# Low parts of split weights and sums of pooled values move from GpSimd to VectorE

## The chip, the core and the metric

The kernel runs on one core of one Trainium2 chip. The metric is the device time of one execution in microseconds (us), the median of several runs. The profile's names are used for the engines: PE is TensorE, DVE is VectorE, ACT is ScalarE, POOL is GpSimd, SP is SyncE, which here issues all DMAs.

## The reference

Three stages follow one another: an attention with two branches over 4 x 8 heads of 576 tokens, and two feed-forward layers over the 2304 tokens of width 512.

```
q_d, k_d, v_d = means over each 4 tokens of q, k, v        # 144 pooled tokens
out_up    = repeat(softmax(q_d k_d^T / 8) v_d, 4)
out_local = softmax(q k^T / 8 where |i - j| < 4) v
x = (out_up + out_local) as [2304, 512]
...
h = x @ w_in                       # moe1, 512 -> 1024
solu = h * softmax(h)
ln = (solu - mean) / sqrt(var + 1e-6) * g_ln
x = ln @ w_out                     # 1024 -> 512
...
h = x @ w_in                       # moe2, 512 -> 2048
out = (h * cos(h)) @ w_out         # 2048 -> 512
```

The four weight matrices arrive as float64, everything else as float32.

## The kernel before

**Products.** The feed-forward products run with float32r operands. Each operand is kept as a high part (its rounded value) and a low part (what is left), and `mm3` makes three matmuls of each product: high by high, high by low, low by high. `split(hi, lo, src, eng)` makes both parts: ACT copies `src` into the high part (line 355), and one subtraction makes the low part (line 356). The subtraction is on DVE, except where `eng=nc.gpsimd` is given, which is so for all four weights.

**Weights on their way in.** `wload` takes a block of a weight by DMA as 64-bit words and makes float32 of it with three integer operations on DVE (lines 393, 395 and 397): the raw words lie in tile `X` (first two weights, blocks of 512 columns) or `wr` (last two weights, blocks of 256 columns), the float32 block in `wu`, a ring of two. Then `split` puts the parts into `R1` (named `R` in the profile: both weights of moe1, later the second weight of moe2) or into `w2i_h` and `w2i_l`. There are 16 blocks of moe1's weights (`w1i_step`, `w1o_step`) and 64 of moe2's (`w2i_step`, `w2o_step`). In `w1o_step` POOL multiplies the block by the layer norm's weight and by 32, the root of 1024 (line 417), before the split.

**Attention.** `Glob` is the pooled branch of a pair of heads, `Loc` the banded one of 192 tokens of a pair. `Glob.prep` sums q and k over four tokens on DVE (line 479) and v on POOL: three additions (line 482) of 72 x 256 elements into `gvs`, 16 times in all. Scores go to PSUM, `softmax` (lines 433 to 440) works on DVE and ACT, PE transposes, and PE multiplies with the values. `Loc.V` adds both branches into `X` on DVE (line 561).

**moe1 and moe2.** `h1_half` is moe1's first product with a maximum on DVE (line 589; two for each 128 tokens, 36 in all), `h1_ln` the softmax and layer norm (its power -1/2 runs on POOL, line 616), `ln_t` the transposes with a split on DVE, `x2` the second product. moe2 goes through 9 groups of 256 tokens and 16 blocks of 128 columns: `h2` (product, cosine in lines 792 to 799, split), and two blocks later `o2`, which adds to the output's banks.

**Order.** The code states what waits for what, and `arrange` then sets the order in which every engine runs its instructions: a list schedule over the whole program on built-in estimates of durations, tried over 14 rounds. Its estimates take each engine by itself. At run time each engine takes its instructions strictly in that order. SP issues DMAs in order as well, so a load that waits for its buffer holds those behind it. `WARM` = 70 matmuls that nobody reads fill gaps of PE at the beginning.

In time, the attention and moe1's weights share the beginning; moe1 and the rest of the attention follow; moe2's weights are brought in alongside the last third of moe1 and the first group of moe2; then moe2 runs alone.

Of the kernel before, what the change touches and what calls it, by code (L numbers as in the profile page):

```python
# [18 lines left out]
FAC = 4              # tokens of a pooled token  # L19
HALO = FAC - 1       # half width of the band  # L20
QB = 64              # queries of a block
WIN = QB + 2 * HALO  # keys of a local block
NB = 3               # blocks of an item
QT = NB * QB         # tokens of a local item
GT = 256             # tokens of a MoE group
W1C, W2C = 512, 256  # columns of the weights' blocks on their way in

# How far, in items, an attention item's steps lie apart: its loads before its scores (a local item's,
# a global one's q and k, its v), its transposes and its values after them.
LEAD, LEAD_QK, LEAD_V, LAG_T, LAG_V = 2, 2, 1, 1, 2  # L30
PACE = 1.1           # steps of moe1 for each attention item
SIDE = 0.55           # blocks of moe1's weights for each attention item
LAG, RING = 2, 4     # moe2: blocks from the first product to the second, places for what lies between
WARM = 70            # matmuls that may fill the tensor engine's first gaps
ROUNDS = 14
# PSUM banks by what they hold
# [5 lines left out]
# ------------------------------------------------------------------------ order of the instructions  # L42
# A list schedule on estimates of what the instructions take settles the order in which each engine runs them.

TO_PE, TO_POOL, TO_ANY = 210.0, 180.0, 135.0  # ns from an engine to another
WRITTEN = {"DVE": 127.0, "Activation": 143.0, "Pool": 127.0}  # from a write to its read by the same engine
DMA_ISSUE, DMA_START, DMA_END, DMA_RATE, DMA_FLIGHT = 475.0, 1100.0, 935.0, 360.0, 8
CLOCK_TICK, CLOCK_COLUMNS = 10240 / 3, 3060.0  # the tensor engine's clock doubles after a tick with so many columns
# [3 lines left out]
class Turns:  # L52
    """A tile pool that keeps account of the tiles that take turns in its slots."""
# [27 lines left out]
def region(o):  # L81
    """An operand's tile, partitions and bytes."""
# [11 lines left out]
class Step:  # L94
    """An instruction, and what it is estimated to take."""
# [205 lines left out]
def kernel(  # L301
# [218 lines left out]
    class Loc:  # L520
# [32 lines left out]
        def V(self):  # L553
            ps = bank("lv")[:, :QT]
            for a in range(NB):
# [10 lines left out]
                op=ALU.add,  # L566
            )

    # --------------------------------------------------------------------- MoE 1
    H = {}  # L570
    TB = 128 // QB  # blocks of 128 tokens

# [314 lines left out]
```

## Time and profile before

| | |
|---|---|
| median of 3 runs | 826.56 us |
| the runs | 819.25, 826.56, 827.91 us |
| span of the profiled execution | 816.9 us |
| time of the profiled execution | not listed; 819.25 us if it was the first run, which leaves 2.4 us outside the span |
| PE busy | 792.9 us, 97% |
| DVE busy | 528.0 us, 65% |
| ACT busy | 473.3 us, 58% |
| POOL busy | 130.6 us, 16% |

The busy shares are means over stages with different limits, so the stretches matter more than the whole. A busy time counts each moment once; the durations of single instructions can overlap a little, since the next one on an engine may begin before the last one's record ends. POOL's spans are rough.

### The profile page before, as it was taken

The numbers are of one execution on the slowest core, as the hardware profiler recorded it, in microseconds if no ns is written. First come the engines' busy times: TensorE is split into PE (matmuls) and PEld (weight loads), VectorE is DVE, ScalarE is ACT, GpSimd is POOL, SyncE is SP. The second block draws the span as 40 slices with busy tenths as digits, with TensorE's granted clock in tenths as the row PEclk, the third lists the DMA queues.
The fourth block names the chain that finished last, engine by engine and source line by source line (L and its number), as shares of the span: only waits on it lengthen the run. The fifth ranks groups of instructions, "written<-read, shape, count | busy, mean of one in ns | idle before, by whom it ended". The sixth has DMA issues, their size and how long they took to land.

```text
span 816.9 us, 15396 instructions
## 1 busy us (share of the span) xinstructions
PE 792.9 (97%) x5894; PEld 672.2 (82%) x5894; DVE 528.0 (65%) x1348; ACT 473.3 (58%) x1366; POOL 130.6 (16%) x172
## 2 busy tenths in 40 slices
PE   6898999999999999999999999999999999999998
PEld 3565768787787887998978999999999999999997
DVE  6987997775747478889999544444445445454443
ACT  3555566665637445455566656565656656565654
POOL 4473342220000013433333000000000000000000
PEclk9977999999999999999999999999999999999999
DMA  9964520401200023332432000000000000000000
GB/s 253 238 167 142 149 76 23 158 17 34 70 18 28 12 68 115 104 116 85 137 116 91 27 1 26 1 27 1 26 2 1 27 1 26 1 27 1 26 1 26
DMA packets 23481, 50.34 MB, mean 62 GB/s; under 512 B 3792, under 2 KB 7664, under 8 KB 23408
## 3 DMA queue, kind: packets, MB, share of 16 engines
q1 hardware_dynamic: 23408, 49.36, 19.6%
q8 instruction: 46, 0.75, 0.4%
q14 instruction: 27, 0.22, 0.1%
HBM read 44.63 MB, written 4.72 MB: 60 GB/s over the span
## 4 chain that ended last, share of the span: by engine, by line
PE 76%; DVE 16%; issue 3%; DMA 2%; ACT 1%; POOL 1%; SPq 0%; POOLq 0%; DVEq 0%; ACTq 0%
PE h2b L361 4%; PE h2b L360 4%; PE h2b L359 4%; PE h2a L360 4%; PE ob L361 4%; PE h2a L359 4%; PE oa L359 4%; PE ob L360 4%; PE oa L360 4%; PE h2a L361 4%; PE ob L359 4%; PE oa L361 4%; PE ls L541 3%; DVE wu L395 3%; PE h L359 3%
## 5 line engine op out<-in xcount | busy, mean ns | idle before, releaser
L356 DVE TENSOR_TENSOR Gl<-t,Gh 128x256 fp32r<-128x256 f32 x144 | 61.5, 427 | 55.8 <-ACT Gh L355 55.8
L355 ACT ACTIVATE Gh<-t 128x256 fp32r<-128x256 f32 x144 | 60.0, 417 | 58.5 <-DVE t L797 58.3
L795 ACT ACTIVATE t<-t 128x256 f32<-128x256 f32 x144 | 60.1, 418 | 55.8 <-DVE t L793 55.6
L359 PE MATMUL x<-Gh,R 128*128 128x256 f32 x288 | 81.8, 286 | 1.7 <-ACT Gh L355 1.5
L360 PE MATMUL x<-Gl,R 128*128 128x256 f32 x288 | 81.8, 285 | 0.7 <-DVE m L596 0.4
L361 PE MATMUL x<-Gh,R 128*128 128x256 f32 x288 | 81.9, 286 | 0.0
L797 DVE SCALAR_TENSOR_TENSOR t<-t,h2b 128x256 f32<-128x256 f32 x72 | 30.2, 420 | 58.2 <-ACT t L796 58.2
L797 DVE SCALAR_TENSOR_TENSOR t<-t,h2a 128x256 f32<-128x256 f32 x72 | 30.2, 420 | 54.2 <-ACT t L796 54.1
L796 ACT ACTIVATE t<-t 128x256 f32<-128x256 f32 x144 | 60.2, 418 | 4.2
L359 PE MATMUL h<-R,xh 128*128 128x512 f32 x144 | 62.3, 433 | 0.3 <-ACT xh L355 0.3
L361 PE MATMUL h<-R,xl 128*128 128x512 f32 x144 | 59.6, 415 | 0.0
L360 PE MATMUL h<-R,xh 128*128 128x512 f32 x144 | 59.0, 410 | 0.0
L359 PE MATMUL oa<-R,Gh 128*128 128x512 f32 x144 | 57.4, 399 | 1.6 <-ACT Gh L355 1.6
L361 PE MATMUL oa<-R,Gl 128*128 128x512 f32 x144 | 56.5, 392 | 1.7 <-DVE Gl L356 1.7
L359 PEld LDWEIGHTS x<-Gh,R 128*128 128x128 f32 x288 | 55.0, 191 | 3.2 <-ACT Gh L355 2.0
L361 PE MATMUL ob<-R,Gl 128*128 128x512 f32 x144 | 57.1, 397 | 0.0
L360 PE MATMUL oa<-R,Gh 128*128 128x512 f32 x144 | 56.9, 395 | 0.0
L360 PEld LDWEIGHTS x<-Gl,R 128*128 128x128 f32 x288 | 55.1, 191 | 2.1 <-DVE Gl L356 1.4
L360 PE MATMUL ob<-R,Gh 128*128 128x512 f32 x144 | 56.6, 393 | 0.0
L436 ACT ACTIVATE le<-ls,sm 128x70 f32<-128x70 f32 x144 | 44.2, 319 | 21.0 <-DVE sm L434 12.2
L359 PE MATMUL ob<-R,Gh 128*128 128x512 f32 x144 | 56.3, 391 | 0.0
L361 PEld LDWEIGHTS x<-Gh,R 128*128 128x128 f32 x288 | 55.0, 191 | 1.0 <-issue 0.6
(120 smaller groups left out, 2284.8 us busy)
## 6 DMA issues: line engine op xcount, KB each, us to landing
wr<-in_w2i_dram SPq DMA_DIRECT2D x32, 256.0 KB
wr<-in_w2o_dram SPq DMA_DIRECT2D x32, 256.0 KB
lv<-in_vl_dram SPq DMA_DIRECT2D x48, 105.0 KB
gv<-in_vg_dram SPq DMA_DIRECT2D x16, 288.0 KB
out_dram<-X SPq DMA_DIRECT2D x18, 256.0 KB
X<-in_w1i_dram SPq DMA_DIRECT2D x8, 512.0 KB
X<-in_w1o_dram SPq DMA_DIRECT2D x8, 512.0 KB
kt<-in_k_dram SPq DMA_DIRECT2D x6, 594.0 KB
```

Of the source, the lines that this page charges most:

```text
L355: nc.scalar.activation(out=hi, in_=src, func=AF.Copy)
L356: (eng or nc.vector).tensor_tensor(out=lo, in0=src, in1=hi.bitcast(F32), op=ALU.subtract)
L359: nc.tensor.matmul(ps, lh, rh, start=start, stop=False)
L360: nc.tensor.matmul(ps, lh, rl, start=False, stop=False)
L361: nc.tensor.matmul(ps, ll, rh, start=False, stop=stop)
L395: nc.vector.scalar_tensor_tensor(out=ui, in0=high, scalar=-0x40000000, in1=ui, op0=ALU.bitwise_and, op1=ALU.bitwise_or)
L436: nc.scalar.activation(out=e[:, j, :], in_=src[:, j, :], func=AF.Exp, bias=neg[:, j:j + 1], scale=scale, accum_out=ssum[:, j:j + 1])
L541: nc.tensor.matmul(o[64 * h:64 * h + 64, :], self.q[:, h, a * QB:(a + 1) * QB], self.k[:, h, a * QB:a * QB + WIN], start=False, stop=a == ...
L795: nc.scalar.activation(out=a, in_=c, func=AF.Sin, scale=0.5)
L796: nc.scalar.activation(out=c, in_=a, func=AF.Square, scale=2.0 ** 0.5)
L797: nc.vector.scalar_tensor_tensor(out=a, in0=c, scalar=1.0, in1=ps, op0=ALU.subtract, op1=ALU.mult, reverse0=True)
```

## The change

Everything that POOL did with two-input arithmetic on large tiles goes to DVE; of the arithmetic POOL keeps only the power of the layer norm.

- The low parts of all 80 weight blocks are made on DVE (`split` no longer has an `eng`).
- In `w1o_step` the multiplication of the block by the layer norm's weight (line 417) is dropped as an instruction. `split` takes the weight as `gain`: ACT copies with a scale per partition, and DVE makes the low part as (src x gain) - high in one instruction. The factor 32 is put into `g_sb` once, by one small DVE instruction.
- The sum over four v tokens becomes two additions on DVE: tokens 0, 1 plus tokens 2, 3 in place (72 x 512 elements), then the two halves (72 x 256).

The rest of the difference removes comments only. Line numbers after the change are four to six higher: 355 becomes 356 (or 359 with a gain), 356 becomes 357 (or 360), 393, 395, 397 become 398, 400, 402, and 482 becomes 485 and 487.

```diff
-    def split(hi, lo, src, eng=None):
-        nc.scalar.activation(out=hi, in_=src, func=AF.Copy)
-        (eng or nc.vector).tensor_tensor(out=lo, in0=src, in1=hi.bitcast(F32), op=ALU.subtract)
+    def split(hi, lo, src, gain=None):
+
+        if gain is None:
+            nc.scalar.activation(out=hi, in_=src, func=AF.Copy)
+            nc.vector.tensor_tensor(out=lo, in0=src, in1=hi.bitcast(F32), op=ALU.subtract)
+        else:
+            nc.scalar.activation(out=hi, in_=src, func=AF.Copy, scale=gain)
+            nc.vector.scalar_tensor_tensor(out=lo, in0=src, scalar=gain, in1=hi.bitcast(F32),
+                                           op0=ALU.mult, op1=ALU.subtract)
...
     def w1i_step(i):
-        split(w1i_h[:, k, f], w1i_l[:, k, f], wload(w1i[k * 128:(k + 1) * 128, f], stage), eng=nc.gpsimd)
+        split(w1i_h[:, k, f], w1i_l[:, k, f], wload(w1i[k * 128:(k + 1) * 128, f], stage))
...
         u = wload(w1o[k * 128:(k + 1) * 128, f], stage)
-        nc.gpsimd.tensor_scalar(out=u, in0=u, scalar1=g_sb[:, k:k + 1], scalar2=DFF ** 0.5, op0=ALU.mult, op1=ALU.mult)
-        split(w1o_h[:, k, f], w1o_l[:, k, f], u, eng=nc.gpsimd)
+        split(w1o_h[:, k, f], w1o_l[:, k, f], u, g_sb[:, k:k + 1])
...
-            for r in range(1, FAC):
-                nc.gpsimd.tensor_tensor(out=vs, in0=self.v[:, :, 0, :] if r == 1 else vs, in1=self.v[:, :, r, :],
-                                        op=ALU.add)
+            nc.vector.tensor_tensor(out=self.v[:, :, 0:2, :], in0=self.v[:, :, 0:2, :], in1=self.v[:, :, 2:4, :],
+                                    op=ALU.add)
+            nc.vector.tensor_tensor(out=vs, in0=self.v[:, :, 0, :], in1=self.v[:, :, 1, :], op=ALU.add)
...
     nc.sync.dma_start(out=g_sb, in_=gln.rearrange("(k p) -> p k", p=128))
+
+    nc.vector.tensor_scalar(out=g_sb, in0=g_sb, scalar1=DFF ** 0.5, scalar2=None, op0=ALU.mult)
...
-        split(w2i_h[:, kk, f], w2i_l[:, kk, f], wload(w2i[kk * 128:(kk + 1) * 128, f], raw2), eng=nc.gpsimd)
+        split(w2i_h[:, kk, f], w2i_l[:, kk, f], wload(w2i[kk * 128:(kk + 1) * 128, f], raw2))
...
-            split(w2o_s[:, j, 0, f], w2o_s[:, j, 1, f], wload(w2o[j * 128:(j + 1) * 128, f], raw2), eng=nc.gpsimd)
+            split(w2o_s[:, j, 0, f], w2o_s[:, j, 1, f], wload(w2o[j * 128:(j + 1) * 128, f], raw2))
```

Since `arrange` plans the whole program anew, the order moves on every engine. Two places matter here. At the beginning, while moe1's first weight comes in, this is POOL's order before (`gvs` and `gv` are the pooled values' sums and their raw tokens, `wu` a float32 block):

```order
L482 TENSOR_TENSOR gvs_298<-gv_271 72x256
L482 TENSOR_TENSOR gvs_298<-gvs_298,gv_271 72x256 x2
L356 TENSOR_TENSOR R1_70<-wu_213,R1_70 128x512
L356 TENSOR_TENSOR R1_70<-wu_258,R1_70 128x512
L482 TENSOR_TENSOR gvs_423<-gv_371 72x256
L482 TENSOR_TENSOR gvs_423<-gvs_423,gv_371 72x256 x2
L356 TENSOR_TENSOR R1_70<-wu_315,R1_70 128x512
```

After the change the same work stands in DVE's order, between the conversions of the next blocks (lines 398 to 402) and the softmax's small steps (`sm`):

```order
L400 SCALAR_TENSOR_TENSOR wu_259<-X_71,wu_259 128x512
L357 TENSOR_TENSOR R1_70<-wu_214,R1_70 128x512
L398 TENSOR_SCALAR wu_314<-X_71 128x512
L442 TENSOR_SCALAR sm_477<-sm_477 128x2
L402 SCALAR_TENSOR_TENSOR wu_259<-X_71,wu_259 128x512
L485 TENSOR_TENSOR gv_370<-gv_370 72x2x256
L485 TENSOR_TENSOR gv_418<-gv_418 72x2x256
L487 TENSOR_TENSOR gvs_422<-gv_370 72x256
L487 TENSOR_TENSOR gvs_442<-gv_418 72x256
L443 RECIPROCAL sm_477<-sm_477 128x2
```

Each low part stands several instructions behind the conversion of its own block, and the sums stand in pairs. The second place is the first group of moe2, while its second weight comes in. DVE's order before:

```order
L393 TENSOR_SCALAR wu_5592<-wr_5593 128x256
L797 SCALAR_TENSOR_TENSOR t_5414<-t_5414,h2b_5444 128x256
L395 SCALAR_TENSOR_TENSOR wu_5592<-wr_5593,wu_5592 128x256
L397 SCALAR_TENSOR_TENSOR wu_5592<-wr_5593,wu_5592 128x256
L356 TENSOR_TENSOR Gl_73<-t_5414,Gh_72 128x256
L793 SCALAR_TENSOR_TENSOR t_5499<-t_5499,h2a_5486 128x256
```

And the order of DVE in the same place after the change:

```order
L400 SCALAR_TENSOR_TENSOR wu_5314<-wr_5315,wu_5314 128x256
L398 TENSOR_SCALAR wu_5322<-wr_5323 128x256
L803 SCALAR_TENSOR_TENSOR t_5217<-t_5217,h2a_5204 128x256
L402 SCALAR_TENSOR_TENSOR wu_5314<-wr_5315,wu_5314 128x256
L799 SCALAR_TENSOR_TENSOR t_5217<-t_5217,h2b_5247 128x256
L357 TENSOR_TENSOR Gl_73<-t_5217,Gh_72 128x256
L400 SCALAR_TENSOR_TENSOR wu_5322<-wr_5323,wu_5322 128x256
L357 TENSOR_TENSOR R1_70<-wu_5314,R1_70 128x256
L402 SCALAR_TENSOR_TENSOR wu_5322<-wr_5323,wu_5322 128x256
```

Here the low part of a block (`R1_70<-wu_5314`) stands three instructions behind the last conversion of that block (line 402), and the next block's conversion has begun ahead of it.

## Rows read from the trace of the kernel before

**Rows 1.** The page: the span and the busy times.
```profile
span 816.9 us, 15396 instructions
...
PE 792.9 (97%) x5894; PEld 672.2 (82%) x5894; DVE 528.0 (65%) x1348; ACT 473.3 (58%) x1366; POOL 130.6 (16%) x172
```

**Rows 2.** Busy us (and instructions) in four stretches, then granted clock, DMA share, GB/s.
```profile
15.00:127.50 112.50, 104.17 (x927) 68.99 (x926) 102.84 (x261) 63.94 (x250) 52.61 (x58) 0.89 0.55 156
127.50:300.00 172.50, 172.50 (x1636) 138.55 (x1636) 109.73 (x341) 98.47 (x355) 16.25 (x24) 1.00 0.14 46
300.00:376.00 76.00, 74.16 (x489) 66.89 (x489) 67.58 (x170) 38.90 (x89) 28.51 (x36) 1.00 0.33 108
376.00:451.00 75.00, 71.17 (x490) 64.27 (x489) 71.80 (x171) 47.20 (x119) 26.63 (x35) 1.00 0.32 106
```

**Rows 3.** Groups on POOL: busy us, mean ns of one, idle before.
```profile
L356 POOL TENSOR_TENSOR w2i_l<-wu,w2i_h 128x256 fp32r<-128x256 f32 x32 | 26.1, 824 | 44.5 <-ACT w2i_h L355 44.4
L482 POOL TENSOR_TENSOR gvs<-gvs,gv 72x256 f32<-72x256 f32 x32 | 26.0, 813 | 1.9
...
L356 POOL TENSOR_TENSOR R<-wu,R 128x512 fp32r<-128x512 f32 x16 | 21.3, 1331 | 17.3 <-ACT R L355 17.3
```

**Rows 4.** Timeline about 397 us, all engines: start us, us, instruction.
```profile
396.37 0.28 DVE L393 TENSOR_SCALAR wu<-wr 128x256 int32<-128x256 int32 x1
...
396.69 0.42 DVE L395 SCALAR_TENSOR_TENSOR wu<-wr,wu 128x256 int32<-128x256 int32 x1
...
396.99 0.73 POOL L356 TENSOR_TENSOR R<-wu,R 128x256 fp32r<-128x256 f32 x1 [1.60 <-ACT R L355]
...
397.15 0.85 DVE L397 SCALAR_TENSOR_TENSOR wu<-wr,wu 128x256 int32<-128x256 int32 x1
...
397.93 0.28 DVE L393 TENSOR_SCALAR wu<-wr 128x256 int32<-128x256 int32 x1
```

**Rows 5.** Timeline about 48 us, in the attention.
```profile
47.83 1.27 POOL L356 TENSOR_TENSOR R<-wu,R 128x512 fp32r<-128x512 f32 x1
48.09 1.04 DVE L438 TENSOR_SCALAR sm<-sm 128x3 f32<-128x3 f32 x1
```

**Rows 6.** Timeline of DVE at the eighth maximum of moe1 (line 589).
```profile
126.85 0.68 DVE L589 TENSOR_REDUCE m<-h 128x1 f32<-128x512 f32 x1
```

**Rows 7.** Groups on DVE from 0 to 140 us.
```profile
L397 DVE SCALAR_TENSOR_TENSOR wu<-X,wu 128x512 int32<-128x512 int32 x16 | 14.6, 911 | 0.0
L395 DVE SCALAR_TENSOR_TENSOR wu<-X,wu 128x512 int32<-128x512 int32 x16 | 12.7, 794 | 0.0
L440 DVE TENSOR_TENSOR le<-le,sm 128x210 f32<-128x210 f32 x20 | 11.6, 578 | 0.1
L438 DVE TENSOR_SCALAR sm<-sm 128x3 f32<-128x3 f32 x26 | 11.4, 439 | 3.6 <-ACT le L436 3.4 <-ACT ge L436 0.2
...
L438 DVE TENSOR_SCALAR sm<-sm 128x2 f32<-128x2 f32 x4 | 3.2, 810 | 0.0
```

**Rows 8.** Groups on DVE from 180 to 298 us, where POOL has little to do.
```profile
L440 DVE TENSOR_TENSOR le<-le,sm 128x210 f32<-128x210 f32 x21 | 7.9, 376 | 0.6
...
L438 DVE TENSOR_SCALAR sm<-sm 128x3 f32<-128x3 f32 x25 | 4.1, 164 | 9.1 <-ACT le L436 7.8 <-ACT ge L436 1.3
...
L356 DVE TENSOR_TENSOR xl<-X,xh 128x512 fp32r<-128x512 f32 x5 | 3.4, 680 | 0.0
```

**Rows 9.** Groups on DVE from 300 to 450 us.
```profile
L397 DVE SCALAR_TENSOR_TENSOR wu<-wr,wu 128x256 int32<-128x256 int32 x64 | 34.6, 545 | 0.8
L395 DVE SCALAR_TENSOR_TENSOR wu<-wr,wu 128x256 int32<-128x256 int32 x63 | 29.4, 472 | 1.1
L393 DVE TENSOR_SCALAR wu<-wr 128x256 int32<-128x256 int32 x62 | 23.7, 386 | 6.4 <-POOL w2i_l L356 4.9 <-DMA wr<-in_w2i_dram 0.9 <-POOL R L356 0.6
```

**Rows 10.** Waits of the whole span: us in total, times, longest.
```profile
DVE Gl L356 <- ACT Gh L355: 58.1, 120, 0.7
...
SPq L469 <- POOL gvs L482: 17.1, 6, 6.4
```

## The prediction

> **What bounds the kernel now.** Start with the busy times: PE is busy for 792.9 of 816.9 us, DVE for 528.0, POOL for 130.6 [rows 1]. Read by itself this says that PE is the bound and that DVE has room. The table by stretch says otherwise [rows 2]. From 127.5 to 300 us PE is busy all 172.5 us and DVE only 109.7: there PE sets the pace. From 15 to 127.5 us DVE is busy 102.84 of 112.5 us, from 300 to 376 us 67.58 of 76, from 376 to 451 us 71.80 of 75. In the last two PE leaves 1.84 and 3.83 us unused, and in the first its granted clock is 0.89 on the mean, that is, it spent some time at the lower of its two levels (1.2 instead of 2.4 GHz). So DVE sets the pace in the beginning and nearly so while moe2's weights come in. Those two stretches are the places to which the change adds DVE work.
>
> The next view is the timeline, with DVE and POOL side by side. At 396.99 us a subtraction starts on POOL and takes 0.73 us, to 397.72. The conversion that starts on DVE at 397.15 takes 0.85 us; the one before it, with as many elements and also two tensor inputs, took 0.42 [rows 4]. At 47.83 us POOL starts one of 1.27 us, to 49.10; a DVE instruction on three columns starts at 48.09 and ends at 49.13, with POOL, after 1.04 us [rows 5]. So a DVE instruction that begins under a POOL instruction waits until POOL is through. What DVE loses in this way is counted as busy, which is why DVE looks full where POOL works.
>
> The Trainium skill, "SBUF — State Buffer", section "SBUF: two separate sides", says that DVE and GpSimd share a pair of SBUF ports as an exclusive lock: whoever starts first has it for its whole instruction, against DVE instructions in a two-port mode or with two SBUF inputs, and the other blocks. The two places above agree. By that rule alone the loss could be as large as POOL's 130.6 busy us; the sum below counts what the groups show, which is a third of it.
>
> **The change part by part.**
>
> *What DVE gets back at the beginning.* Compare DVE's groups up to 140 us [rows 7] with the same shapes where POOL is nearly idle [rows 8]: line 397, 16 x (911 - 680) = 3.7 us, with the 512 columns and two inputs of the `xl` row as the clean value; line 395, 16 x (794 - 680) = 1.8; line 440, 20 x (578 - 376) = 4.0; line 438, 26 x (439 - 164) = 7.2 and, on two columns, 4 x (810 - 164) = 2.6. These are 19.3 us. Other groups, line 393 among them, are stretched too and not counted; I take 22, with 19 and 25 as ends.
>
> *What DVE gets there.* The place that ends this stretch is the eighth maximum of moe1, at 126.85 + 0.68 = 127.5 us [rows 6]. In the new order all 16 low parts of moe1's weights and eight of the 16 pairs of value sums stand ahead of it on DVE. Low parts: 16 x 680 ns = 10.9 us [rows 8]. The multiplication by the gain is in the same pass, like the conversions of lines 395 and 397, so no more than that. Sums: 512 columns at 680 ns and 256 at 420 [rows 4, 8], 8 x 1.10 = 8.8 us. Together 19.7 us. A DVE instruction that waits for nothing starts about 0.07 us before the last one's record ends (397.15 + 0.85 against 397.93 [rows 4]), which is 2.2 us for 32 instructions. Net: 19.7 - 2.2 - 22 = **-4.5 us**, with ends of -7.5 and +0.7 (25 back and all of the overlap; 19 back and no overlap). The other eight pairs come where DVE is idle for 63 of 172.5 us [rows 2]: nothing, unless that room goes, when they cost 8.8 us.
>
> *The second weights.* Back, from 300 to 450 us: line 397, 64 x (545 - 420) = 8.0; line 395, 63 x (472 - 420) = 3.3; line 393, 62 x (386 - 280) = 6.6 [rows 9], with the clean values of the timeline [rows 4]: 17.9 us, and some more in shapes not shown. Added: 64 low parts x 420 ns, less 0.07 of overlap each, = 22.4 us. From 376 us on, a block takes 397.93 - 396.37 = 1.56 us on DVE, of which 0.43 is the block by POOL [rows 4]; afterwards it takes 1.56 - 0.43 + 0.35 = 1.48. For 32 blocks that is **-2.6 us**. From 300 to 376 us the other 32 add 11.2 us and get back what is left, 17.9 - 13.8 = 4.1 or somewhat more: 5 to 7 us more on DVE. That is covered by the 8.4 us in which DVE is idle there [rows 2]: 0, and up to +7 if the idle time lies in the wrong places. So the subtraction costs DVE hardly more by doing it than it cost DVE by waiting for POOL.
>
> *What else moves.* A subtraction or addition on POOL took 0.73 to 1.33 us [rows 3, 4], so whatever waits for a low part or a sum gets it earlier. The multiplication of line 417 goes from the path of a block of moe1's second weight; the scale on ACT's copy and the small instruction on `g_sb` I cost at nothing, covered by POOL's missing step; without that cover it is one short instruction on DVE. The pooled values' next load waits on SP for the sums (17.1 us in 6 waits [rows 10]), and behind it stand loads of local values and raw weights. It waits for DVE from now on; sums late in DVE's order would make those loads late. SP has such waits today without PE standing still from 127.5 us on, so 0, with up to +3 in the beginning.
>
> *The plan.* The order is planned on clean durations. Today DVE falls behind it by every blocked instruction, and engines in fixed order then wait for one another: DVE is idle for 9.7 us from 15 to 127.5 us, and PE for 5.7 us from 300 to 451 us [rows 2]. Afterwards the run should keep closer to its plan. How much of these 15.4 us returns no row tells; I take **-3**, with 0 and -15 as ends.
>
> The sum is -4.5 - 2.6 - 3 = -10.1 us. The page lists no time of its own for the profiled execution, only its span of 816.9 us; the lowest of the runs, 819.25, fits it best, and the median is 826.56. I put the change against the median: **816.5 us**. What lies outside the span I leave as it is.
>
> **The rivals.**
>
> *Faster still.* Most of the divergence from the plan goes: -4.5 - 2.6 - 15 = -22 us, 804.5 us. For it: the lower clock between 15 and 127.5 us belongs to the same stalls. Against: loads and scores have waits of their own there, which POOL has no part in.
>
> *No change.* What DVE gains at the beginning is taken by another limit: by PE, which was granted a mean clock of 0.89 there and whose work was merely shifted, or by loads. Only what PE has done when it becomes the bound at 127.5 us counts in the end. Then -0 to -3 us remain: 824 to 829 us.
>
> *Slower: DVE waits for ACT.* POOL could wait for ACT's copy of a block; DVE now stands in that place, and everything behind it on DVE waits too: softmax steps, `Gl`, the next conversions, and PE behind them. The comparable wait of today, DVE's `Gl` for ACT's `Gh`, takes 58.1 us in 120 times, 0.48 each [rows 10]. For 64 low parts this would be 31 us, less the 1.4 to 3.4 us of idle time that is left in the first of the two stretches; with the gain of 10 that gives about 845 us. It decides from some 0.2 us for each low part. Against it: in the new order at least two instructions stand between the last conversion of a block and its low part, in all but 2 of 64 cases.
>
> *Slower: DVE's work was worth sparing.* If the stretched records had another reason than POOL, nothing would come back: +17.5 us less 9.7 idle at the beginning, +22.4 less 8.4 and 3.2 later, +18.6 in all, 845 us. The ends that fall together with POOL's speak against it [rows 4, 5]. The Trainium skill, "Perfetto Trace Analysis", section "Optimizing Scalar/DVE Operations", advises to give work of a saturated DVE to ACT or even GpSimd, which speaks against this change, and adds that for GpSimd the shared read port may undo the gain. By its first half the time would be this rival's.
>
> **How the numbers follow.** The forecast, 811 to 822 us, gets 0.45; faster still 0.14; no change 0.26; DVE waiting for ACT 0.11; no blocking 0.04. About 1% (8.3 us) is what a measurement of this kernel can tell from no change, so faster means below 818.3 us: two thirds of the forecast's range, 0.29, and the second case, 0.43 in all. Slower means above 834.8: 0.15. The rest is 0.42. The range that leaves out both slower cases and the far tail of the fast one is 804 to 831 us.
>
> **What would show it.** In the new profile POOL's busy time falls to under 20 us, and DVE's stays within 15 us of 528: 10.9 + 16 x 1.10 + 64 x 0.42 = 55 us come on top, 8 of them in overlap, and 40 or more go. Lines 398, 400 and 402 have means near 280, 420 and 420 ns on 256 columns and 680 for the two on 512; line 442 has one near 164 ns from the start. The eighth maximum of moe1 (line 593 now) ends near 122 us, and PE is idle for less than 5.7 us while moe2's weights come in. If DVE waits for ACT's copies by more than some 0.2 us each, the third rival was right. If the eighth maximum comes earlier and the end does not, the second was. The largest unknown is the return of the plan: clock levels at the beginning can move it by several us either way.

## The result, and the profile after

The first comparison gave a median of 801.16 us after the change (four runs, 797.35 to 803.61) against 827.14 before (four runs, three of them from 826.56 to 827.91): a ratio of 0.9715, 95% interval 0.9652 to 0.9777. My range ended at 804.

Three more comparisons of the same two kernels came with the experiments, each on another chip: 0.9891 (0.984 to 0.9941), 0.9842 (0.9801 to 0.9884) and 0.9805 (0.9759 to 0.9852). In all, 22 runs after the change have a median of 803.9 us (797.26 to 813.64). 109 runs of the kernel before, beside the experiments, have one of 818.2 us (809.52 to 834.91), and only 6 of the 109 reach 826.5. Without the 12 of all these runs that lie over 1.5% above the fastest beside them, the medians are 803.9 and 817.9 us. So the change is worth about 14 us, and the first comparison showed the kernel before at its slow end.

The page after, as [rows 1]:

```profile
span 801.4 us, 15354 instructions
...
PE 783.0 (98%) x5894; PEld 669.9 (84%) x5894; DVE 523.4 (65%) x1461; ACT 473.0 (59%) x1366; POOL 18.2 (2%) x36
```

POOL lost 112 us of work. DVE took over 113 instructions more and is busy 4.6 us less. The same stretches as [rows 2] (busy us and instructions of PE, PEld, DVE, ACT and POOL; granted clock; DMA share; GB/s):

```profile
15.00:127.50 112.50, 105.24 (x982) 74.17 (x980) 96.87 (x288) 66.73 (x251) 1.48 (x2) 0.93 0.48 141
127.50:300.00 172.50, 172.50 (x1644) 137.97 (x1639) 119.45 (x377) 100.28 (x362) 6.70 (x9) 1.00 0.19 58
300.00:376.00 76.00, 76.00 (x515) 69.88 (x514) 71.17 (x205) 40.77 (x92) 5.56 (x7) 1.00 0.33 103
376.00:451.00 75.00, 75.00 (x517) 69.77 (x516) 66.67 (x197) 50.52 (x134) 0.00 (x0) 1.00 0.35 107
```

PE no longer stands still from 300 to 451 us, and it runs 1032 matmuls there where it ran 979. DVE's groups from 0 to 140 us (answering to [rows 7]) have the clean values now:

```profile
L402 DVE SCALAR_TENSOR_TENSOR wu<-X,wu 128x512 int32<-128x512 int32 x16 | 10.7, 682 | 0.0
L400 DVE SCALAR_TENSOR_TENSOR wu<-X,wu 128x512 int32<-128x512 int32 x16 | 10.7, 676 | 0.0
...
L444 DVE TENSOR_TENSOR le<-le,sm 128x210 f32<-128x210 f32 x20 | 7.4, 371 | 0.0
...
L485 DVE TENSOR_TENSOR gv<-gv 72x512 f32<-72x512 f32 x10 | 6.8, 679 | 3.0 <-DMA gv<-in_vg_dram 3.0
...
L360 DVE SCALAR_TENSOR_TENSOR R<-wu,g_sb,R 128x512 fp32r<-128x512 f32 x8 | 5.8, 744 | 0.0
L357 DVE TENSOR_TENSOR R<-wu,R 128x512 fp32r<-128x512 f32 x8 | 5.5, 682 | 1.0 <-ACT R L356 1.0
...
L442 DVE TENSOR_SCALAR sm<-sm 128x3 f32<-128x3 f32 x27 | 4.3, 161 | 3.7 <-ACT le L440 3.5 <-ACT ge L440 0.2
```

And from 300 to 450 us (answering to [rows 9]):

```profile
L402 DVE SCALAR_TENSOR_TENSOR wu<-wr,wu 128x256 int32<-128x256 int32 x60 | 25.0, 419 | 0.0
L400 DVE SCALAR_TENSOR_TENSOR wu<-wr,wu 128x256 int32<-128x256 int32 x60 | 24.9, 420 | 0.4
L398 DVE TENSOR_SCALAR wu<-wr 128x256 int32<-128x256 int32 x60 | 17.3, 289 | 2.0 <-DMA wr<-in_w2i_dram 1.3 <-DMA wr<-in_w2o_dram 0.3
L357 DVE TENSOR_TENSOR R<-wu,R 128x256 fp32r<-128x256 f32 x32 | 13.3, 419 | 0.1
L357 DVE TENSOR_TENSOR w2i_l<-wu,w2i_h 128x256 fp32r<-128x256 f32 x29 | 12.1, 418 | 0.4 <-ACT w2i_h L356 0.4
```

The last column settles a rival at once: in this stretch the low parts waited for ACT's copies for 0.1 + 0.4 us in all, not for 0.2 us each.

**Where the time went.** Two events divide the span: the 24th maximum of moe1 (lines 589 and 593) and the output copy that ends the second group of moe2 (lines 812 and 818). In between moe2's weights come in. The timelines give before:

```profile
297.99 0.69 DVE L589 TENSOR_REDUCE m<-h 128x1 f32<-128x512 f32 x1 [0.16 <-PE h L361]
...
499.37 0.58 ACT L812 COPY X<-ob 128x512 f32<-128x512 f32 x1
```

and after:

```profile
291.85 0.68 DVE L593 TENSOR_REDUCE m<-h 128x1 f32<-128x512 f32 x1
...
483.59 0.58 ACT L818 COPY X<-ob 128x512 f32<-128x512 f32 x1
```

The ends are 298.68 and 499.95 us before, 292.53 and 484.17 after. So the stretch between them fell from 201.3 to 191.6 us (**-9.6**), and the one ahead of it from 298.7 to 292.5 (**-6.2**). Behind it both kernels take the same time to 0.3 us. The stretch between the two events, before and then after (columns as in [rows 2]):

```profile
298.68:499.95 201.27, 195.60 (x1298) 176.84 (x1297) 163.98 (x398) 117.94 (x286) 55.14 (x71) 1.00 0.25 83
...
292.53:484.17 191.64, 191.64 (x1296) 176.90 (x1295) 161.08 (x461) 116.09 (x286) 5.56 (x7) 1.00 0.28 87
```

PE is busy in all of it after the change, at the full clock: there it is the bound. Before, it idles for 5.7 us and is busy 4.0 us longer with as many matmuls (a few records are missing). DVE runs 63 instructions more after the change and is busy 2.9 us less.

The first stretch differs from run to run, the second hardly: the three other profiled executions of the changed kernel have 191.4, 191.5 and 191.6 for the second, and 293.5, 297.7 and 286.8 for the first. Every experiment is read by these two. The ratios are those of the comparisons; a difference given with an experiment below is worked out from its ratio and 818.2 us. (For the first three parts the plain differences of medians, against 819.29 us beside them, are 1.6 to 2.4 us larger.)

| kernel | median us | ratio to before (95%) | to the 24th maximum | from there to the second output |
|---|---|---|---|---|
| before | 818.2 | | 298.7 | 201.3 |
| before again | 817.88 | 0.9997 (0.9964 to 1.003) | 313.3 | 201.3 |
| after | 803.9 | 0.9715, 0.9891, 0.9842, 0.9805 | 292.5 | 191.6 |
| before, moe2's low parts moved | 808.6 | 0.9896 (0.9845 to 0.9948) | 298.1 | 191.4 |
| before, moe1's low parts moved | 814.3 | 0.9968 (0.9938 to 0.9998) | 293.0 | 200.3 |
| before, sums moved | 808.8 | 0.9892 (0.9858 to 0.9926) | 289.3 | 201.6 |
| after, unread POOL work late | 818.96 | 1.0019 (0.998 to 1.0058) | 291.8 | 209.0 |
| after, unread POOL work early | 815.29 | 0.9972 (0.9935 to 1.001) | 301.5 | 191.2 |
| before, plan told of stretched conversions | 812.7 | 0.9939 (0.991 to 0.9967) | 303.9 | 190.8 |
| after, same plan (now mistold) | 814.06 | 0.9969 (0.9939 to 0.9998) | 293.1 | 202.2 |
| before, plan told of softmax steps too | 823.07 | 1.005 (1.0023 to 1.0077) | 310.7 | 190.8 |
| before, all moved but moe1's low parts | 801.14, 801.37 | 0.979, 0.9816 | 289.7 | 191.4 |
| after, slower loads in the plan | 802.92 | 0.9792 (0.9751 to 0.9832) | 292.0 | 190.2 |
| before, 200 fill matmuls | 833.83 | 1.0197 (1.0167 to 1.0228) | 315.6 | 200.7 |
| after, 200 fill matmuls | 812.45 | 0.9938 (0.9918 to 0.9959) | 301.0 | 192.1 |
| after, half of moe1's low parts on POOL | 798.22 | 0.9774 (0.9738 to 0.9811) | 284.4 | 191.4 |

(The last two columns are those of one profiled execution each.)

### The profile page after: what moved, and what is told of

The parts are those of the page before. It is cut to its first block, busy times and chain, and to the rows that moved or that the text cites. A ratio compares the mean times of both kernels' runs of the same rounds, so it can differ in the third digit from the quotient of the medians.

```text
span 801.4 us, 15354 instructions
## 1 busy us (share of the span) xinstructions
PE 783.0 (98%) x5894; PEld 669.9 (84%) x5894; DVE 523.4 (65%) x1461; ACT 473.0 (59%) x1366; POOL 18.2 (2%) x36
## 3 DMA queue, kind: packets, MB, share of 16 engines
q1 hardware_dynamic: 23408, 49.36, 19.9%
## 4 chain that ended last, share of the span: by engine, by line
PE 94%; DVE 2%; DMA 2%; ACT 1%; issue 0%; SPq 0%; DVEq 0%; ACTq 0%
PE h L364 5%; PE x L364 5%; PE x L365 4%; PE h2b L366 4%; PE x L366 4%; PE h2a L365 4%; PE h2a L364 4%; PE h2b L365 4%; PE h2b L364 4%; PE h2a L366 4%; PE h L366 4%; PE oa L364 4%; PE ob L366 4%; PE oa L365 4%; PE h L365 4%; PE ob L365 4%
```

## Experiments: the parts by themselves

The theory was the prediction's: POOL blocks DVE, and what DVE does in POOL's place costs it no more than the blocking; the rest is the return of the plan. The rival was that the parts work through something else, by earlier low parts and sums.

**The kernel before, unchanged.** 

> The kernel before, unchanged, run once more. It shows how far its executions spread and how much of the difference between the two profiled spans (816.9 against 801.4 us) is the execution that was profiled. If the beginning, with its falls of the granted clock, is what varies, the eighth maximum of moe1 ends elsewhere than at 127.5 us and the stretch from 300 us on takes as long as before. Ratio 1.00 within 0.01.

It gave 817.88 us, 0.9997 of before. Its profiled execution took 833.33 us: the granted clock was at its lower level from 39.1 us for 30.7 us and from 104.0 us for 37.5 us. Yet the second stretch lasted 201.3 us, to the tenth as in the other trace. What varies from run to run is the beginning.

**moe2's low parts alone.** In the kernel before, `eng=nc.gpsimd` is dropped in two places.

```diff
-        split(w2i_h[:, kk, f], w2i_l[:, kk, f], wload(w2i[kk * 128:(kk + 1) * 128, f], raw2), eng=nc.gpsimd)
+        split(w2i_h[:, kk, f], w2i_l[:, kk, f], wload(w2i[kk * 128:(kk + 1) * 128, f], raw2))
...
-            split(w2o_s[:, j, 0, f], w2o_s[:, j, 1, f], wload(w2o[j * 128:(j + 1) * 128, f], raw2), eng=nc.gpsimd)
+            split(w2o_s[:, j, 0, f], w2o_s[:, j, 1, f], wload(w2o[j * 128:(j + 1) * 128, f], raw2))
```

> The kernel before, with the 64 low parts of moe2's weights on DVE and nothing else moved. Blocking theory: POOL no longer holds DVE up from 300 us on, PE's idle time there (5.7 us) goes, and the run gains 8 to 11 us, with the beginning as it was. Rival (the new plan as a whole gives the gain, by luck of the order): no relation to the stretch; 0 or the whole 23. Rival (DVE's work counts): slower by up to 10 us.

808.6 us, -8.5. The second stretch is 191.4 us: the late part of the gain, whole.

**moe1's low parts alone**, the gain included, with sums and moe2's low parts left on POOL.

```diff
-        split(w1i_h[:, k, f], w1i_l[:, k, f], wload(w1i[k * 128:(k + 1) * 128, f], stage), eng=nc.gpsimd)
+        split(w1i_h[:, k, f], w1i_l[:, k, f], wload(w1i[k * 128:(k + 1) * 128, f], stage))
...
-        nc.gpsimd.tensor_scalar(out=u, in0=u, scalar1=g_sb[:, k:k + 1], scalar2=DFF ** 0.5, op0=ALU.mult, op1=ALU.mult)
-        split(w1o_h[:, k, f], w1o_l[:, k, f], u, eng=nc.gpsimd)
+        split(w1o_h[:, k, f], w1o_l[:, k, f], u, g_sb[:, k:k + 1])
```

> Only moe1's 16 low parts on DVE, with the gain in the second one's split; sums of pooled values and moe2's weights on POOL as before. Blocking theory: the beginning gets shorter by 2 to 8 us, since 11 us of DVE work come and some 10 to 12 us of blocked time and the multiplication of line 417 go; from 300 us on as before. Rival (order): anything.

814.3 us, -2.6, with an interval that ends at 0.9998.

**The sums alone.** The kernel before with the two additions of lines 485 and 487 on DVE.

```diff
-            for r in range(1, FAC):
-                nc.gpsimd.tensor_tensor(out=vs, in0=self.v[:, :, 0, :] if r == 1 else vs, in1=self.v[:, :, r, :],
-                                        op=ALU.add)
+            nc.vector.tensor_tensor(out=self.v[:, :, 0:2, :], in0=self.v[:, :, 0:2, :], in1=self.v[:, :, 2:4, :],
+                                    op=ALU.add)
+            nc.vector.tensor_tensor(out=vs, in0=self.v[:, :, 0, :], in1=self.v[:, :, 1, :], op=ALU.add)
```

> Only the sums of pooled values on DVE, as two additions instead of three. Blocking theory: 38 us of POOL work go, a third of it falling on DVE as blocked time (10 to 13 us), for 17.6 us on DVE of which 9 stand ahead of the eighth maximum: 2 to 8 us faster. Rival (DVE's work counts): 5 us slower or more.

808.8 us, -8.8, all of it up to the 24th maximum; the eighth maximum ends at 117.9 us instead of 127.5. The three add up to some -20 us, against a typical -14 for the whole: by themselves they do not add.

**All but moe1's low parts**: the diffs of the first and the third part together.

> The kernel before with the sums of the pooled values and the low parts of moe2's 64 blocks on DVE; the 16 low parts and 8 multiplications of moe1's blocks stay on POOL. If the parts add up (-8.9 and -8.5 us alone), the ratio is near 0.979, some 802 us. If DVE becomes the bound once the sums are on it, and POOL's 27 us of moe1's blocks still block it, part of the 8.9 us goes: 0.985 or more. If the first weights on POOL matter no more, it equals the changed kernel, 0.972.

0.979: these two add up as expected (0.9896 x 0.9892 = 0.9789). The comparison left it open whether the remaining part helps at all, so it was made again beside the changed kernel.

> The kernel of the run with all but the first weights moved, again, now on one chip with the changed kernel: moe1's 16 low parts and 8 multiplications on POOL, all else as after the change. Alone on the kernel before, moving them gave 2.6 us. If that holds here too, this kernel is 2 to 4 us slower than the changed one. If DVE is what is short up to the eighth maximum once the sums are on it, it is 2 to 5 us faster (801.14 against 805.2 us on one chip in two separate comparisons), and the eighth maximum stands near 114 us against 126.

> The changed kernel unchanged, as the reference on this chip: between 0.9715 and 0.9891 of before.

801.37 us (0.9783 to 0.985) against 801.86 (0.9759 to 0.9852): no difference. Once the sums and moe2's low parts are moved, it does not show in the time where moe1's 16 low parts are made. With the eight of the first weight on POOL and the others on DVE, from the changed kernel:

```diff
-        split(w1i_h[:, k, f], w1i_l[:, k, f], wload(w1i[k * 128:(k + 1) * 128, f], stage))
+        u = wload(w1i[k * 128:(k + 1) * 128, f], stage)
+        nc.scalar.activation(out=w1i_h[:, k, f], in_=u, func=AF.Copy)
+        nc.gpsimd.tensor_tensor(out=w1i_l[:, k, f], in0=u, in1=w1i_h[:, k, f].bitcast(F32), op=ALU.subtract)
```

> The changed kernel with the 8 low parts of moe1's first weight back on POOL (8 x 1.33 us there, 8 x 0.68 us off DVE); those of its second weight stay on DVE with the gain. If DVE's time up to the eighth maximum decides, it lies between the other two, nearer to the one with all 16 on POOL as the first weight comes first; if blocking decides, it is slower than the changed kernel by 1 to 2 us.

798.22 us (0.9738 to 0.9811): the lowest median of all, though its interval overlaps those of the other two, so I can't call it better. Neither of the two cases expected came true.

## Experiments: is it the blocking?

If DVE loses time because POOL works, then POOL work that nobody reads must bring the loss back into the changed kernel. It was added outside of the plan, so that PE, DVE, ACT and SP keep their order of instructions. Here 64 subtractions of 128 x 256, one behind each block of moe2's weights:

```diff
+    def ghost(hi, lo, n):
+        g = moe.tile([128, 256], BF16, tag="ghost", name="ghost", bufs=1)[:, :n]
+        nc.gpsimd.tensor_tensor(out=g, in0=lo.bitcast(F32), in1=hi.bitcast(F32), op=ALU.subtract)
...
+    steps = [x for x in steps if not any(o.bass_ap.tensor.name.startswith("ghost") for o in tiles(x.outs))]
...
+        ghost(w2i_h[:, kk, f], w2i_l[:, kk, f], W2C)
...
+            ghost(w2o_s[:, j, 0, f], w2o_s[:, j, 1, f], W2C)
```

> The changed kernel, and for each of moe2's 64 weight blocks one more subtraction on POOL, which starts when DVE has made the low part, reads both parts and writes a scratch tile that nobody reads. The output is the same, and so is the order on PE, DVE, ACT and SP. Blocking theory: DVE is held up by up to 0.43 us each time again, 15 to 27 us in a stretch in which DVE has some 13 us of idle time, so PE gets idle time there and the run is 8 to 20 us slower than the changed kernel (ratio to the kernel before 0.98 to 0.995). Rival (what helped is that nobody waits for POOL's result any more): nobody waits for these either, so the time is that of the changed kernel, ratio 0.97.

The time is 818.96 us: the whole gain is gone. Windows and DVE's groups (300 to 450 us) of this kernel:

```profile
300.00:376.00 76.00, 70.44 (x448) 63.02 (x447) 74.50 (x186) 37.00 (x84) 26.05 (x34) 0.98 0.32 98
376.00:451.00 75.00, 69.94 (x484) 64.69 (x483) 73.75 (x186) 44.14 (x113) 25.78 (x33) 0.98 0.35 106
```

```profile
L408 DVE SCALAR_TENSOR_TENSOR wu<-wr,wu 128x256 int32<-128x256 int32 x57 | 27.7, 488 | 0.0
L406 DVE SCALAR_TENSOR_TENSOR wu<-wr,wu 128x256 int32<-128x256 int32 x57 | 27.0, 478 | 0.4
L404 DVE TENSOR_SCALAR wu<-wr 128x256 int32<-128x256 int32 x58 | 24.2, 417 | 0.8 <-DMA wr<-in_w2i_dram 0.4
```

Line 404 does what line 398 did, in 417 ns instead of 289; DVE is busy 148 of 151 us, and PE now idles 10.6 us. The second stretch grew by 17.3 us, to 209.0. Some 3 us of that go with the granted clock (an estimate: 0.98 in both windows, so 2% of 151 us). No instruction reads this work, and the layer norm's power, which shares POOL with it, is not late by it: DVE waited 3.3 us for the power in the whole run, 3.7 in the changed kernel. So it is the presence of the work on POOL that does this. The same at the beginning, with 16 subtractions and 48 additions:

```diff
+        ghost(w1i_h[:, k, f], w1i_l[:, k, f], W1C)
...
+        ghost(w1o_h[:, k, f], w1o_l[:, k, f], W1C)
...
+            for _ in range(FAC - 1):
+                g = moe.tile([128, 448], BF16, tag="ghost", name="ghost", bufs=1)
+                nc.gpsimd.tensor_tensor(out=g[:SH, :256], in0=vs.rearrange("p a d -> p (a d)"),
+                                        in1=vs.rearrange("p a d -> p (a d)"), op=ALU.add)
```

> The changed kernel, and POOL instructions that nobody reads in the attention: one subtraction of 128 x 448 elements for each of moe1's 16 blocks and three additions of 72 x 256 for each of the 16 sums. The order on the other engines is that of the changed kernel, the output too. Blocking theory: the lines of the softmax and of the conversions are stretched again (line 442 on the mean to 300 ns or more), the eighth maximum comes 5 to 15 us later, ratio 0.98 to 0.99. Rival (shorter chain, or two additions instead of three): no change from 0.97.

815.29 us, about 11 more than the changed kernel, and this time the second stretch stays at 191.2 and the first grows to 301.5. The conversions on 512 columns take 842 ns (682 without), line 450 (the changed kernel's 442) 255 ns instead of 161.

## Experiments: is it the plan?

POOL's work is the same in the next kernel as before the change, and on POOL. Only the estimates of DVE's conversions in the plan are the stretched means of the trace, less the 64 ns of overlap.

```diff
+            if out.bass_ap.tensor.name.startswith("wu") and "int32" in str(out.dtype):
+                means = {256: (386.0, 472.0, 545.0), 512: (580.0, 794.0, 911.0)}[n]
...
+                return means[kind3] - 64.0
```

> The kernel before, all work on the engines of before, but the list schedule is told for the conversions of weights what they took on the mean in the trace of before (386, 472, 545 ns on 256 columns; 580, 794, 911 on 512; less 64 of overlap). If the gain of the change is mostly that DVE keeps to its plan, a plan that knows the blocked time gets part of it: 3 to 8 us from 300 us on. If it is the blocked time itself, 0 within 3 us.

```profile
300.00:376.00 76.00, 76.00 (x503) 69.37 (x502) 67.23 (x169) 39.77 (x92) 26.90 (x35) 1.00 0.34 106
376.00:451.00 75.00, 74.81 (x542) 70.69 (x541) 69.09 (x180) 50.51 (x129) 28.88 (x35) 1.00 0.38 114
```

POOL still works for 55.8 us in these windows and DVE is busy 136.3 us, against 139.4 [rows 2], but PE hardly idles, and the second stretch is 190.8 us. DVE's groups from 300 to 450 us show that its conversions are still stretched, though less than in [rows 9]:

```profile
L403 DVE SCALAR_TENSOR_TENSOR wu<-wr,wu 128x256 int32<-128x256 int32 x62 | 31.0, 504 | 0.2
L401 DVE SCALAR_TENSOR_TENSOR wu<-wr,wu 128x256 int32<-128x256 int32 x62 | 29.0, 476 | 0.3
L399 DVE TENSOR_SCALAR wu<-wr 128x256 int32<-128x256 int32 x63 | 19.8, 319 | 3.6 <-POOL w2i_l L362 1.3 <-ACT sq L615 1.0 <-POOL R L362 0.6
```

An order that knows of the blocking gets the late gain of the change without the change. It does so in two ways that this run does not separate: it allows for blocked instructions, and it has fewer of them (between the two events DVE is busy 155.3 us with 393 instructions, against 164.0 with 398). That it is no lucky order is likely from the other plans: four plans of kernels with this work on POOL that knew nothing of the blocking have 200.3 to 201.6 us there, the two that were told have 190.8. In the other direction, the changed kernel with the same lines added, which are wrong for it:

> The changed kernel, and the same too long estimates, which are now wrong by 55 us in all. If keeping to the plan is what matters, 3 to 10 us slower than the changed kernel (ratio 0.975 to 0.985). If only the work and the blocking matter, 0.97 as the changed kernel.

```profile
300.00:376.00 76.00, 73.93 (x495) 67.74 (x495) 65.46 (x191) 37.85 (x87) 3.93 (x6) 1.00 0.31 98
376.00:451.00 75.00, 69.73 (x477) 62.48 (x475) 65.99 (x196) 46.19 (x121) 1.04 (x2) 1.00 0.35 106
```

202.2 us, with next to nothing on POOL and DVE at 131.5 of 151 us; between the two events DVE is busy 161.3 us, as in the changed kernel (161.1). A part of what is lost shows in DVE's groups: the low parts now wait for ACT.

```profile
L363 DVE TENSOR_TENSOR R<-wu,R 128x256 fp32r<-128x256 f32 x30 | 12.5, 420 | 3.9 <-ACT R L362 3.9
L363 DVE TENSOR_TENSOR w2i_l<-wu,w2i_h 128x256 fp32r<-128x256 f32 x29 | 11.8, 419 | 5.6 <-ACT w2i_h L362 5.6
```

That is the wait of my third rival, 9.5 us of it. It comes with a wrong plan, not with the change.

**The beginning too?** The same was tried for the softmax steps of the beginning: 439, 810 and 578 ns for lines 438 and 440.

```diff
+            if name.startswith("sm_") and "TensorScalar" in kind and n > 1:
...
+                    if LATER["softmaxes"] <= 30:
+                        return (439.0 if n == 3 else 810.0) - 64.0
+            if name.startswith(("le_", "ge_")) and n == 210 and len(self.ins) > 1:
...
+                    return 578.0 - 64.0
```

> The kernel before, whose plan is told the stretched means of the conversions (as in the run told of those alone, 812.7 us) and now also those of the beginning's softmax steps: 439 ns for the first 26 of line 438 on three columns, 810 for the four on two, 578 for the first 20 of line 440. Engines and work stay as before. If the loss at the beginning is a matter of the plan, as it was while moe2's weights come in, the 24th maximum of moe1 comes near 292 us as after the change (298.7 before) and the time is 803 to 807 us. If the loss at the beginning is DVE's time itself (102.84 of 112.5 us busy there), which no order gives back, the 24th maximum stays at 298 us or later and the time near 812 us.

823.07 us, worse than before the change. The second stretch is again 190.8, but the eighth maximum ends at 138.7 us and the 24th at 310.7. At the beginning neither of the two plans that were told makes up for the blocking. Why is open. It is not shown that DVE's time is what is short there: in the window that has DVE busy for 102.84 of 112.5 us before [rows 2], this run has it busy for 93.60, at a lower granted clock, 0.83 on the mean.

```profile
15.00:127.50 112.50, 101.47 (x842) 68.48 (x842) 93.60 (x227) 58.92 (x224) 52.41 (x54) 0.83 0.50 149
```


**Loads.** The plan assumes 360 bytes per ns for loads, the page shows 270 GB/s in the first slice.

```diff
-DMA_ISSUE, DMA_START, DMA_END, DMA_RATE, DMA_FLIGHT = 475.0, 1100.0, 935.0, 360.0, 8
+DMA_ISSUE, DMA_START, DMA_END, DMA_RATE, DMA_FLIGHT = 475.0, 1100.0, 935.0, 264.0, 8
```

> The changed kernel with one number of the plan altered: it assumes 264 bytes per ns for loads instead of 360; the page of the changed kernel shows 270 GB/s in the first slice of the span, where loads are all there is to do. If the plan at the beginning loses by loads that land later than it thinks (in the groups up to 140 us DVE waits 3.6, 3.0 and 1.5 us for loads of k, v and q), the first 125 us get shorter by 2 to 5 us: 796 to 799 us, the ratio to before near 0.967. If loads have slack there, no change: 0.969 to 0.975. From the second output on the same time in both.

802.92 us, no change that can be told.

## Experiments: what spreads the beginning?

> The changed kernel unchanged, beside many runs of the kernel before. If the three runs of 826.6 to 827.9 us of the kernel before were the slow end of its spread at the beginning (its 22, 31 and 17 runs beside the other experiments have medians of 818.4 to 819.3), the ratio is that of the parts alone, (818.4 - 20.0) / 818.4 = 0.976, some 799 us, and the early part of the gain is near 6 us as in the two profiled executions. If the first comparison was typical, 0.9715 and an early part of about 14 us.

0.9891, a smaller gain than either case expected, with the second stretch at 191.4. So the first comparison was not typical, and the beginning of the changed kernel spreads as well. Where its clock falls, the windows show what came ahead. Before:

```profile
34.70:39.70 5.00, 3.13 (x38) 1.84 (x37) 5.00 (x11) 1.79 (x5) 2.13 (x3) 1.00 0.94 216
39.70:49.90 10.20, 10.20 (x54) 6.21 (x54) 6.97 (x19) 5.25 (x23) 5.16 (x6) 0.50 0.64 155
```

After:

```profile
59.70:64.70 5.00, 3.65 (x44) 2.39 (x42) 5.00 (x17) 2.37 (x10) 0.00 (x0) 1.00 0.36 111
64.70:74.90 10.20, 10.03 (x58) 6.67 (x54) 8.58 (x29) 7.21 (x28) 0.93 (x1) 0.50 0.66 218
```

In both, DVE is busy all of the 5 us ahead and PE 3.1 or 3.7 us of them; then PE runs at a granted clock of 0.50, 1.2 GHz, for 10.2 us. To take the falls away, the fill matmuls were raised from 70 to 200 in both kernels.

```diff
-WARM = 70
+WARM = 200
```

> The kernel before with 200 instead of 70 matmuls that nobody reads; in its order the last of them stands after 776 rows of PE. In the traces the 70 are used up at 34 us (before) and 41 us (after), and the granted clock falls to its lower level later than that: at 39.7, 67.0 and 104.5 us in the kernel before, at 64.7 us in the one after. If these falls spread the beginning from run to run and chip to chip, and fill prevents them, the falls after 34 us go and the time is 5 to 10 us shorter, with a narrower spread (by now 809.5 to 834.9). If fill only pushes real work back (each takes 0.2 to 0.3 us of PE), the time is the same or longer, 818 to 830.

> The changed kernel with 200 matmuls of fill. By the theory that falls of the granted clock make the first comparison (0.9715) and the second (0.9891) differ: the fall at 64.7 us goes, 793 to 799 us with a narrow spread, and against the kernel before with the same fill the gain is that of the two profiled executions without what the falls gave, 10 to 16 us. By the rival that fill pushes real work back: 803 to 815.

> The changed kernel unchanged, on the chip of the two runs with more fill. Together with the first two comparisons it tells whether chips differ: if they do, the ratio lies between 0.9715 and 0.9891 and the clocks of before and after go with it; the stretch from the 24th maximum to the second group's output is 191 to 192 us whatever the ratio (201.2 before).

The changed kernel on that chip took 805.2 us (0.9842), with 191.5 us for the second stretch. With more fill its runs lie between 808.97 and 814.13, all twelve at a mean clock of 0.993 to 0.998, where the 22 without it spread from 797 to 814 at 0.972 to 0.995. Its granted clock by slices:

```profile
PEclk9899999999999999999999999999999999999999
```

The kernel before with more fill has five runs from 831.25 to 834.99 us, at 0.987 to 0.995, and one of 843.83 at 0.971. So the spread does go with the clock. But both kernels get longer, the one before by 16 us, the changed one by 7 to 9, and the fill pushes real work back: before, the eighth maximum ends at 193.7 us instead of 127.5. The rival was right about the time, and for the kernel before it fell short. A second sign is in the runs without more fill: among the 109 of the kernel before, the 12 with a mean clock below 0.975 have a median of 826.5 us, the 45 from 0.979 to 0.982 one of 817.4, and the 9 from 0.987 to 0.990 one of 813.8; of the changed kernel, 806.2 (5 runs) and 802.5 (4 runs) at the last two clocks. At equal clock the change gives 11 us. The remaining 3 go with the clock, whose mean is higher in the changed kernel (median 0.985 of its 22 runs, 0.979 of the 109); that the clock is their cause is not shown. Why some runs have more falls than others stays open.

## Why the prediction was off

**What bounds the kernel** was read rightly. Unread POOL work alone stretches the DVE instructions and takes the gain away in both stretches.

**The gain at the beginning** (-4.5) fits what many runs give: -14.3 in all, less the 9.6 of the second stretch, is -4.7. DVE's terms fit too: the groups of [rows 7] and line 393 got back 22.1 us (22 taken), and low parts and sums took 19.9 us ahead of the eighth maximum (19.7 taken). That the gain fits with them is in part luck. The place that I named for it was less sure: the eighth maximum ended at 125.8 us, later than 122, and at 126.7, 130.9 and 120.0 us in the other executions. The parts are not as I split them either. The sums carry it (-8.8 alone), and moe1's low parts on DVE add nothing to them.

**The second weights** (-2.6) were right as DVE's own time: low parts at 419 ns, conversions at 289, 420 and 419, and between the two events DVE is busy 2.9 us less than before.

**The plan** (-3, ends 0 and -15) is the step that failed: the mechanism was right, the term too small. The late part of the gain is 9.6 us; less the 2.6 that I gave to DVE's own time, 7.0 are left for the plan, more than twice my term for both stretches. I took the PE idle time in that stretch, 5.7 us [rows 2], as what could return, and a fraction of it as likely. All of it returned, and 4.0 us more, by which PE is busy longer before for as many matmuls: idle time alone understated what PE lost. Runs show that the order can be worth that much: telling the plan of the stretched conversions gives 10.4 us (201.3 to 190.8) with POOL's work left in place, and mistelling it costs 10.6 (191.6 to 202.2) with next to none. How the 9.6 us divide between blocked time and order is not shown, since the order that was told is also blocked less. This is the rival *faster still*, for the late stretch; it had a chance of 0.14.

**The base** was the second step that failed: the sum was put against the median of three runs, 826.56, where the terms come from a profiled execution with a span of 816.9 us, which the lowest run, 819.25, fits best. Of the 15.3 us between 816.5 and 801.16, 8.3 are that base (818.2 in 109 runs), 4.2 the sum (-10.1 for -14.3), and 2.7 the first four runs of the changed kernel (803.9 in 22). From the usual 818.2 the same sum gives 808.1 us.

**No change** spoke of the beginning's gain being taken by another limit. For moe1's low parts no gain shows once the others are moved; for the sums it does not hold. **DVE waits for ACT** is out: 0.5 us late and 1.0 at the beginning. **No blocking** is out. Of the section that spoke against the change, in the Trainium skill's "Perfetto Trace Analysis", "Optimizing Scalar/DVE Operations", the second half holds here, that the shared read port may undo what giving DVE's work to GpSimd gains: taking the work back was worth 14 us.

## What to carry to other kernels

Two engines that block one another cost twice: the blocked time itself, and what a fixed order planned without it makes of it. Before an engine is relieved by moving its work, compare the same instruction with and without the other engine at work; where an order is planned ahead, feed the plan with the durations measured in that mix, which here brought the late gain by itself, though not the early one. And take a prediction's base from the same execution as its terms: three runs of a kernel whose clock falls at the beginning can lie 8 us from its usual time.

## What the runs showed of the hardware

- Even a DVE instruction on three columns is held by a POOL instruction on large tiles. In the kernel before, ten of line 438 on three columns began under a subtraction or an addition of POOL, after the fashion of [rows 5]: nine ended 24 to 31 ns after it, the tenth later. The 49 that met no POOL arithmetic took 162 ns on the mean. Not every DVE instruction is held. The reciprocal behind it (line 439), on the same columns, began under POOL work 12 times and never took more than 177 ns. All of both lines in the kernel before (min/median/max in ns):

```profile
L438 DVE TENSOR_SCALAR sm<-sm x68: 135/162/1914, 12.2 to 285.1; 128x3 f32<-128x3 f32 x60, 128x1 f32<-128x1 f32 x4, 128x2 f32<-128x2 f32 x4
L439 DVE RECIPROCAL sm<-sm x68: 147/166/177, 12.6 to 285.3; 128x3 f32<-128x3 f32 x60, 128x1 f32<-128x1 f32 x4, 128x2 f32<-128x2 f32 x4
```

  After the change line 438's successor, line 442, never takes more than 172 ns. The sum of line 479, with one input from SBUF (the on-chip memory), is not held either: five of its 16 began under POOL work and took 1.32 to 1.34 us, the 16 together 1.32 to 1.36.
- A factor per partition is not free. DVE's pass of line 360 takes 744 ns with it, line 357 on as many elements 682. On ACT the copy of line 359 takes 720 ns with the factor, that of line 356 630, in the groups of ACT from 0 to 140 us after the change:

```profile
L359 ACT ACTIVATE R<-wu,g_sb 128x512 fp32r<-128x512 f32 x8 | 5.7, 720 | 1.6 <-DVE wu L402 1.5
L356 ACT ACTIVATE R<-wu 128x512 fp32r<-128x512 f32 x8 | 5.0, 630 | 2.3 <-DVE wu L402 2.3
```

- The beginning of one and the same program spreads by some 25 us from run to run, with the granted clock, while the 190 to 200 us behind the 24th maximum repeat to a few tenths of a microsecond for the same kernel (191.4 to 191.6 in four executions after, 201.3 twice before).
